# First loads of a fused attention and feed-forward kernel on one queue, with one warming matmul less

## The chip, the cores and the metric

One core of one Trainium2 chip. The metric is device time in microseconds (us) of one execution; the time given for a kernel is a median over runs. The profile is of one execution, and its span runs from the first to the last instruction.

Five engines run side by side, each with its own list of instructions, and meet by semaphores: TensorE (PE in the profile, PEld for its weight loads), VectorE (DVE), ScalarE (ACT), GpSimd (POOL) and SyncE (SP). SyncE and ScalarE also issue DMA transfers, each on a queue of its own (SPq and ACTq in the profile; q1 and q10 in its list of queues).

## The reference

The input x is 2048 rows by 512. A linear attention with 32 heads of width 16 and a feed-forward layer with 1376 hidden columns are both computed from it and mixed by a gate:

```
g = sigmoid((x * gate_w).sum(-1, keepdims=True))
q, k, v = heads(x @ wqkv)
phi(t) = concat(softmax(t @ w_phi), softmax(-(t @ w_phi)))     # per head, for q and k
kv, z = phi(k)^T v, phi(k) summed over rows
a = (phi(q) @ kv / (phi(q) @ z + 1e-6)) @ wo
b = relu(x @ w1) @ w2
out = g * a + (1 - g) * b
```

All inputs and the output are bf16.

## The kernel before, in words

Rows are worked on in tiles of 128 (16 of them) and in chunks of 512 (4 of them). The hidden layer h = relu(x @ w1) is made transposed, in 11 blocks of 128 hidden columns for each chunk. The products q and k use weights that are folded with w_phi first: `pe_fold` (L408) multiplies a transposed weight (WT, which the DMA transposes wkT and wqT fill) by a block-diagonal mask of w_phi (WBD, made on VectorE at L363 from the load wphi).

Each piece of work is a named task with an engine, the tasks that it depends on, and a closure that emits its instructions. The order on each engine is written out by hand in the table `ORDER` at the top: a list of task names for each engine. A task waits only for the semaphores of its dependencies; everything behind a waiting task on its engine waits with it. `emit` puts the waits and the instructions out in that order. The fields `dur` and `lat` belong to a planner that isn't run here, and do nothing.

The start of the program is what the change touches. The names:

- `warm0` (L292), on PE: six matmuls of 512 columns on a constant, into a PSUM bank that is overwritten later. They wait for nothing but the constant.
- `x00` to `x03` (issued at L306): the four 128-row tiles of x's first chunk, 128 KB each, into a piece of the tile FT (it is called XN in the code). `xt00`, `xt01` and so on (L384) transpose each tile on PE by the identity matrix, two 128-column blocks a task. `xe00`, `xe10`, `xe20`, `xe30` (L396, ScalarE) and `xe01` to `xe31` (L399, VectorE) evict those to XT.
- `w1a0` to `w1a3` (L306): the four 128-row blocks of w1, each cut to its first 512 columns, 128 KB each, into the tile W1 (the profile shortens names, so W1 and W2 both appear as W there). `w1b` is columns 512 to 1023 of all four row blocks, `w1c` the rest.
- `hh00`, `hh01` (row block 0, tile 0 and tile 1 of x), `hh1` (row block 1), `hh2` (row block 2), `hh3` and `hh4` (row block 3, two halves), all at L439: the first part of h on PE, for the first 256 rows of x. `hh00` and `hh01` have four matmuls of 128 columns each, `hh1` and `hh2` four of 256, `hh3` and `hh4` two of 256. `hr0`, `hr1` and `h0_0` to `h0_3` (L445) finish those four column blocks, `h0_4` and on (L425) do whole blocks; `h0_4` is the first to need `w1b`.
- `f1_0` to `f1_3` (L408): the folds for k, which need `wkT` and the masks. `h1_0` (L425) is the first matmul group that needs `x1`, the DMA transpose (L311) of x's second chunk, and `x1` is issued only when `w1c` has landed.

PE's order there is: warm0, xt00, xt01, xt10, xt11, hh00, hh01, hh1, hh2, xt20, xt21, hh3, xt30, xt31, hh4, hr0, hr1, h0_0 to h0_5, f1_0 to f1_3, h0_6. SyncE issues x00, w1a0, w1a2, x02, x03, w1b, wphi, wkT, w1c, wv, x1 and on; ScalarE begins with x01, w1a1, w1a3 and then the evictions. Before ScalarE's first activation there is a table load (ACT_TABLE_LOAD in the profile), which stands where that activation stands.

Of the kernel before, what the change touches and what calls it, by code (L numbers as in the profile page):

```python
# [5 lines left out]
ACT = mybir.ActivationFunctionType  # L6
# [9 lines left out]

ORDER = {
# [4 lines left out]
    ),  # L22
# [5 lines left out]
    ),  # L28
    "act": (
# [153 lines left out]
def bass_gated_mix__linear_kernel_hedgehog__dense_activation_relu__prompt_kernel(  # L183
# [11 lines left out]
    x2 = A_x.rearrange("b s d -> (b s) d")  # L195
# [4 lines left out]
    P = 128  # L200
# [14 lines left out]
    NPH, NOM, NOT, NOS = 7, 3, 4, 5  # L215
    NDB, AB = (6, 7), (3, 4, 5, 2)
    GATE_LIMIT = 40.0
    WARM = (6 * (512,),)
    RL = 400.0
    FE = "dve"  # L220

    with ExitStack() as es:
        E = es.enter_context

        def sb(name, shape, dt):
            return E(nc.sbuf_tensor(name, shape, dt))
# [6 lines left out]
        W1 = sb("W1", [P, ND, W1C], BF16)  # L233
# [30 lines left out]
        EP = sb("EP", [P, NT], FP32)  # L264
# [7 lines left out]
        def psap(off, dims):  # L272
# [3 lines left out]
        add = g.add  # L276
# [5 lines left out]
            boost=700.0)  # L282
# [4 lines left out]
        one = nc.const_aps.tensor(1.0, (P, 1), BF16).tensor  # L287
        ones_w, ones_m = (bass.AP(tensor=one, offset=0, ap=[[1, P], [0, n]]) for n in (P, 512))

        def pe_warm(q, cols):  # L290
            for n in cols:
                last = q.matmul(PS[:, 2, 0:n], ones_w, ones_m[:, 0:n], start=True, stop=True)  # L292
            return last

        for n, cols in enumerate(WARM):
            add(f"warm{n}", "pe", lambda q, c=cols: pe_warm(q, c), (), dur=sum(cols) / 1200.0, boost=3000.0)
# [3 lines left out]
        def after_last(name, eng):  # L300
            if eng in queue:
                g.follow(queue[eng], name)
            queue[eng] = name

        def load(name, eng, out_, in_, deps=(), dur=0.1, lat=6.0, **how):
            add(name, eng, lambda q: q.dma_start(out=out_, in_=in_, **how), deps, dur=dur, lat=lat, dma=True,  # L306
                boost=1e4)
            after_last(name, eng)
# [9 lines left out]
        w1r = B_w1.rearrange("(j p) n -> p j n", p=P)  # L318
        x0r = x2[chunk(0), :].rearrange("(m p) d -> p m d", p=P)
        wvr = A_wqkv[:, 2 * D:3 * D].rearrange("(j p) n -> p j n", p=P)  # L320
        def load_x(m, eng, lat):
            load(f"x0{m}", eng, XN[:, m, :], x0r[:, m, :], dur=0.45, lat=lat)

        def load_w(j, eng, lat):
            load(f"w1a{j}", eng, W1[:, j, 0:512], w1r[:, j, 0:512], dur=0.45, lat=lat)

        load_x(0, "sp", 2.95)
        load_x(1, "act", 3.1)
        load_w(0, "sp", 3.2)
        load_w(1, "act", 3.4)  # L330
        load_w(2, "sp", 3.8)
        load_w(3, "act", 3.95)
        load_x(2, "sp", 4.0)
        load_x(3, "sp", 3.9)
        load("w1b", "sp", W1[:, :, 512:1024], w1r[:, :, 512:1024], dur=0.5, lat=5.0)
# [52 lines left out]
        for m in range(4):  # L388
# [3 lines left out]
            for n, eng in enumerate(("act", "dve")):  # L392
                xo = XT[:, 2 * n:2 * n + 2, m * P:(m + 1) * P]
                xi = PS[:, XB[m][n], 0:2 * P].rearrange("p (j t) -> p j t", j=2)
                if eng == "act":
                    add(f"xe{m}{n}", eng, lambda q, o=xo, i=xi: q.activation(o, i, ACT.Copy), (f"xt{m}{n}",), dur=0.35,  # L396
                        boost=9000.0 - 10 * m)
                else:
                    add(f"xe{m}{n}", eng, lambda q, o=xo, i=xi: q.tensor_copy(o, i), (f"xt{m}{n}",), dur=0.37,  # L399
                        boost=9000.0 - 10 * m)  # L400
# [36 lines left out]
        def pe_h_first(q, j, c0, c1, ks=range(4)):  # L437
            for k in ks:
                last = q.matmul(PS[:, GB4[k], c0:c1], W1[:, j, k * P:(k + 1) * P], XT[:, j, c0:c1],  # L439
                                start=(j == 0 and c0 == 0), stop=(j == ND - 1), skip_group_check=True)  # L440
            return last
# [11 lines left out]
        prev = "hh01"  # L453
        for n, (j, ks) in enumerate(((1, range(4)), (2, range(4)), (3, (0, 1)), (3, (2, 3)))):
            add(f"hh{n + 1}", "pe", lambda q, j=j, ks=ks: pe_h_first(q, j, 0, 2 * P, ks),
                (f"xe0{j // 2}", f"xe1{j // 2}", f"w1a{j}", prev), dur=0.11 * len(ks), boost=8500.0)
            prev = f"hh{n + 1}"

        for k in range(2):
            add(f"hr{k}", "pe", lambda q, k=k: pe_h_rest(q, k, 2 * P, 3 * P, True), ("xe20", "xe21", prev), dur=0.22,  # L460
                boost=8200.0)
            prev = f"hr{k}"
# [13 lines left out]
        for n, (kind, a, k) in enumerate(units):  # L476
            b = GB4[n] if n < 4 else FB[2] if n == 4 else HB[(n - 4) % len(HB)]
            if kind == "h":
                halved = n < 4
                deps = [*xof[a], *w1of[k], prev, *freed[b]]  # L480
                if k == KT - 1:
                    deps.append("gw")
                    add(f"h{a}_{k}", "pe", lambda q, a=a, b=b: pe_h_tail(q, a, b), deps, dur=0.69)
                    prev = f"h{a}_{k}"
# [15 lines left out]
                    deps, dur=(0.22 if k < 2 else 0.44) if halved else 0.87,  # L500
                    boost=8000.0 if n < 3 else 0.0)
                prev = f"h{a}_{k}"
# [3 lines left out]
            else:  # L506
                deps = ["wqT", *wbd, prev, *freed[b]]
                add(f"f{a}_{k}", "pe", lambda q, a=a, k=k, b=b: pe_fold(q, a, k, b), deps, dur=0.24, boost=1000.0)
                prev = f"f{a}_{k}"
# [4 lines left out]
        for j in range(ND):  # L514
# [3 lines left out]
                boost=1800.0)  # L518
# [11 lines left out]
        for m in range(NT):  # L530
            def add(*a, boost=20.0 * (len(widths) * 2 - m // 2 - VLAG), **how):
                return g.add(*a, boost=boost, **how)
# [17 lines left out]
        for jn, (kind, tiles) in enumerate(jobs):  # L550
# [66 lines left out]
            else:  # L617
# [4 lines left out]
                    dur=0.11 + 0.207 * w)  # L622
# [24 lines left out]
                for m in tiles:  # L647
# [39 lines left out]
                    if m == NT - 1:  # L687
# [3 lines left out]
                        prev = None  # L691
                        for h2 in range(2):
# [12 lines left out]
                            prev = f"a{m}_{h2}"  # L705
# [12 lines left out]
                            else:  # L718
                                add(f"oe{m}_1", "dve", lambda q, m=m, b=b, cs=cs: q.tensor_scalar(  # L719
                                    OSB[:, m % NOS, cs], PS[:, b, 0:cs.stop - cs.start], OMG[:, m:m + 1], None, ALU.mult), need,  # L720
                                    dur=0.4)
                            add(f"st{m}_{h2}", ("act", "sp")[h2], lambda q, m=m, cs=cs: q.dma_start(
                                out=o2[m * P:(m + 1) * P, cs], in_=OSB[:, m % NOS, cs]), (f"oe{m}_{h2}",), dur=0.5,
                                lat=1.5, dma=True)
# [55 lines left out]
```

## Time and profile before

| | us |
|---|---|
| median of 3 runs | 150.16 (150.09 to 150.39) |
| the profiled execution | 149.87 |
| its span | 148.3 |
| TensorE busy | 145.5 |
| VectorE busy | 111.7 |
| GpSimd busy | 109.6 |
| ScalarE busy | 91.4 |

How to read it: the busy times are of single engines and overlap. "L292" is a line of the kernel. In a list in order of time, a row gives the start, the length of the stretch, the engine (with a q for its sequencer, which issues DMAs), the line, the operation, the tile written and the tiles read, the number of instructions merged into the row, and in brackets the idle time of the engine ahead of it with what ended it. The ends of matmuls are modelled and overlap the next start, so the starts are the safer numbers. For a DMA the duration on the issuing engine is the time to issue it; the time from there to its landing is listed in another view, the DMA view.

### The profile page before, as it was taken

What the parts mean: (1) busy time and instruction counts of PE and PEld (TensorE: products, weight loads), DVE (VectorE), ACT (ScalarE), POOL (GpSimd) and SP (SyncE); (2) the same over time, 40 slices, a digit from 0 to 9 for tenths busy, and PEclk for the clock granted to TensorE, in tenths of its full rate; (3) what the DMA queues carried; (4) which work ended last, traced back from release to release, by engine and by line L of the source; (5) the groups of instructions that cost most, each with busy time, mean ns of one, the idle gap of its engine ahead of it and who ended that gap; (6) DMA issues with size and microseconds to landing.
All of it is one profiled execution on the core that took longest, in us unless ns stands there. A gap on an engine that the chain in (4) does not pass through costs nothing.

```text
span 148.3 us, 2542 instructions
## 1 busy us (share of the span) xinstructions
PE 145.5 (98%) x1009; PEld 75.3 (51%) x1009; DVE 111.7 (75%) x169; ACT 91.4 (62%) x126; POOL 109.6 (74%) x72
## 2 busy tenths in 40 slices
PE   7999999999999999999999999999999999999994
PEld 2875444445654475445444545455444444445453
DVE  2433666998896948989999997999999988634502
ACT  3475769799969765898983937175583751310141
POOL 4000499999999999999999999999999793150000
PEclk9999999999999999999999999999999999999999
DMA  4998999910040001000000093646957785556752
GB/s 139 324 256 220 169 187 214 340 51 4 0 73 0 0 4 38 0 0 4 0 0 0 7 141 71 141 95 138 183 119 167 180 214 116 141 134 158 64 157 92
DMA packets 46363, 16.11 MB, mean 109 GB/s; under 512 B 39856, under 2 KB 46352, under 8 KB 46352
## 3 DMA queue, kind: packets, MB, share of 16 engines
q1 hardware_dynamic: 43760, 13.61, 42.6%
q10 hardware_dynamic: 2592, 2.34, 4.9%
q8 instruction: 8, 0.13, 0.4%
q14 instruction: 3, 0.02, 0.1%
HBM read 4.41 MB, written 2.10 MB: 44 GB/s over the span
## 4 chain that ended last, share of the span: by engine, by line
PE 98%; DVE 0%; issue 0%
PE PS L676 24%; PE PS L425 21%; PE PS L545 19%; PE PS L526 9%; PE PS L682 9%; PE PS L611 3%; PE PS L654 3%; PE PS L433 2%; PE PS L292 2%; PE PS L698 2%; PE PS L439 2%; PE PS L445 1%; PE PS L408 1%; PE PS L384 1%; PE PS L709 1%; DVE OSB L719 0%
## 5 line engine op out<-in xcount | busy, mean ns | idle before, releaser
L590 POOL TENSOR_TENSOR TS<-PB,MX 128x1024 bf16<-128x1024 bf16 (+1 forms) x18 | 30.9, 1723 | 14.5 <-DVE MX L581 14.5
L676 PE MATMUL PS<-W,HT 128*128 128x512 bf16 (+1 forms) x165 | 38.1, 379 | 0.0
L597 DVE TENSOR_REDUCE ZB<-FT 128x128 f32<-128x2048 bf16 (+1 forms) x18 | 36.6, 2031 | 1.8 <-ACT FT L595 1.8
L595 ACT ACTIVATE FT<-TS 128x2048 bf16<-128x2048 bf16 (+1 forms) x18 | 30.9, 1718 | 9.6 <-POOL TS L590 9.5
L425 PE MATMUL PS<-XT,W 128*128 128x512 bf16 x144 | 34.7, 379 | 0.0
L590 POOL TENSOR_TENSOR TS<-MN,PB 128x1024 bf16<-128x1024 bf16 (+1 forms) x18 | 30.9, 1726 | 0.8 <-DVE MN L583 0.8
L545 PE MATMUL PS<-WP,XT 128*128 128x512 bf16 x128 | 30.6, 379 | 0.0
L604 POOL TENSOR_TENSOR FT<-FT,SC 128x2048 bf16<-128x2048 bf16 (+1 forms) x9 | 29.6, 3293 | 0.0
L503 ACT ACTIVATE HT<-PS 128x512 bf16<-128x512 f32 x40 | 22.6, 597 | 5.4 <-PE PS L425 4.6
L581 DVE TENSOR_REDUCE MX<-PB 128x64 bf16<-128x1024 bf16 (+1 forms) x18 | 19.5, 1085 | 5.9 <-ACT PB L577 5.9
L676 PEld LDWEIGHTS PS<-W,HT 128*128 128x128 bf16 (+1 forms) x165 | 15.4, 98 | 16.9
L730 ACT ACTIVATE OSB<-PS,OMG 128x512 bf16<-128x512 f32 x14 | 9.6, 686 | 21.1 <-PE PS L682 20.5
L583 DVE TENSOR_REDUCE MN<-PB 128x64 bf16<-128x1024 bf16 (+1 forms) x18 | 19.3, 1084 | 3.2 <-ACT PB L577 3.2
L425 PEld LDWEIGHTS PS<-XT,W 128*128 128x128 bf16 x144 | 13.7, 98 | 15.4
L577 ACT ACTIVATE PB<-PS 128x1024 bf16<-128x1024 f32 (+1 forms) x18 | 16.7, 927 | 7.2 <-PE PS L545 4.0
L545 PEld LDWEIGHTS PS<-WP,XT 128*128 128x128 bf16 x128 | 12.1, 98 | 13.5
L526 PE MATMUL PS<-WV,XT 128*128 128x512 bf16 x64 | 16.4, 379 | 0.0
L627 POOL TENSOR_TENSOR FT<-FT,SR 128x1024 bf16<-128x1024 bf16 (+1 forms) x9 | 15.7, 1740 | 0.7
L682 PE MATMUL PS<-WO,OT 128*128 128x512 bf16 x60 | 14.9, 378 | 0.0
L663 DVE SCALAR_TENSOR_TENSOR OTM<-PS,EG,RD 128x256 bf16<-128x256 f32 x32 | 13.8, 463 | 0.2
L661 DVE RECIPROCAL RD<-PS 128x16 f32<-128x16 f32 x32 | 6.4, 232 | 9.0 <-PE PS L654 8.8
L535 ACT ACTIVATE VS<-PS 128x512 bf16<-128x512 f32 x16 | 9.6, 602 | 4.3 <-PE PS L526 4.3
(55 smaller groups left out, 106.6 us busy)
## 6 DMA issues: line engine op xcount, KB each, us to landing
out_dram<-OSB ACTq DMA_DIRECT2D x14, 128.0 KB, 2.2
W<-in_B_w_dram SPq DMA_DIRECT2D x1, 1280.0 KB, 7.5
W<-in_B_w_dram SPq DMA_DIRECT2D x1, 512.0 KB, 4.5
WV<-in_A_wqkv_dram SPq DMA_DIRECT2D x1, 512.0 KB, 4.9
WO<-in_A_wo_dram SPq DMA_DIRECT2D x1, 512.0 KB, 7.5
FT<-in_A_x_dram SPq DMA_DIRECT2D x3, 128.0 KB, 3.1
W<-in_B_w_dram SPq DMA_DIRECT2D x1, 352.0 KB, 4.1
W<-in_B_w_dram ACTq DMA_DIRECT2D x2, 128.0 KB, 3.3
```

The source lines that it names most:

```text
L425: last = q.matmul(PS[:, b, :], W1[:, j, k * P:(k + 1) * P], XT[:, j, chunk(c)], start=(j == 0), stop=(j == ND - 1))
L503: add(f"rl{a}_{k}", "act", lambda q, a=a, k=k, b=b: q.activation(HT[:, k, chunk(a)], PS[:, b, :], ACT.Relu), (prev,), dur=0.6, boost=RL)
L526: last = q.matmul(PS[:, 2, :], XT[:, j, m * P:(m + 1) * P], WV[:, j, :], start=(j == 0), stop=(j == ND - 1))
L545: last = q.matmul(PS[:, n, :], XT[:, j, m * P:(m + 1) * P], WP[:, s, j, :], start=(j == 0), stop=(j == ND - 1))
L581: add(f"mx_{J}", "dve", lambda q, sl=sl, w=w, i=pbg: q.tensor_reduce(MX[:, sl, 0:w * H], i, AX.X, ALU.max), (f"ev_{J}", old("t1")), dur=0. ...
L583: add(f"mn_{J}", "dve", lambda q, sl=sl, w=w, i=pbg: q.tensor_reduce(MN[:, sl, 0:w * H], i, AX.X, ALU.min), (f"ev_{J}", old("t2")), dur=0. ...
L590: add(f"{tn}_{J}", "pool", lambda q, o3=o3, a3=a3, b3=b3: q.tensor_tensor(o3, a3, b3, ALU.subtract), (f"{'mx' if sg == 0 else 'mn'}_{J}", ...
L595: add(f"ex_{J}", "act", lambda q, fs=fs, ts=ts, w=w: q.activation(FT[:, fs, 0:w * F], TS[:, ts, 0:w * F], ACT.Exp), (f"t1_{J}", f"t2_{J}", ...
L597: add(f"sm_{J}", "dve", lambda q, fs=fs, sl=sl, w=w: q.tensor_reduce(ZB[:, sl, 0:2 * w * H], FT[:, fs, 0:w * F].rearrange("p (g d) -> p g ...
L604: add(f"nm_{J}", "pool", lambda q, f3=f3, sl=sl, w=w: q.tensor_tensor(f3, f3, SC[:, sl, 0:2 * w * H].unsqueeze(2).to_broadcast([P, 2 * w * ...
L676: last = q.matmul(PS[:, ab, :], HT[0:r, k, m * P:(m + 1) * P], W2[0:r, k, :], start=(k == 0), stop=False)
L682: last = q.matmul(PS[:, ab, :], OT[:, m % NOT, t, :], WO[:, t, :], start=False, stop=(t == ND - 1))
```

## The change

SyncE issues all of the first loads, and ScalarE none. w1a2 and w1a3 become one load of 256 KB, which keeps the name w1a2; hh3 and hh4 wait for it as hh2 does. SyncE's order is then x00, x01, w1a0, w1a1, w1a2, x02, x03, w1b, and the rest as it was. ScalarE begins with a new task, `first`: an activation that copies one column of a constant into a column of EP, which is written again before it is read. It waits for nothing. warm0 has five matmuls instead of six.

```diff
     "sp": (
-        "x00 w1a0 w1a2 x02 x03 w1b wphi wkT w1c wv x1 x2 wqT x3 gw w2a w2b wo hx0 hx1 hx2 tq0 tq1 "
+        "x00 x01 w1a0 w1a1 w1a2 x02 x03 w1b wphi wkT w1c wv x1 x2 wqT x3 gw w2a w2b wo hx0 hx1 hx2 tq0 tq1 "
...
     "act": (
-        "x01 w1a1 w1a3 xe00 xe10 xe20 xe30 rl0_0 rl0_1 rl0_3 rl0_2 rl0_4 fe1_1 fe1_3 rl0_5 ev_k0 rl0_8 rl0_6 "
+        "first xe00 xe10 xe20 xe30 rl0_0 rl0_1 rl0_3 rl0_2 rl0_4 fe1_1 fe1_3 rl0_5 ev_k0 rl0_8 rl0_6 "
...
-    WARM = (6 * (512,),)
+    WARM = (5 * (512,),)
...
         load_x(0, "sp", 2.95)
-        load_x(1, "act", 3.1)
+        load_x(1, "sp", 3.1)
         load_w(0, "sp", 3.2)
-        load_w(1, "act", 3.4)
-        load_w(2, "sp", 3.8)
-        load_w(3, "act", 3.95)
+        load_w(1, "sp", 3.4)
+        load("w1a2", "sp", W1[:, 2:4, 0:512], w1r[:, 2:4, 0:512], dur=0.45, lat=3.8)
+        add("first", "act", lambda q: q.activation(EP[:, 0:1], bass.AP(tensor=one, offset=0, ap=[[1, P], [1, 1]]), ACT.Copy),
+            (), dur=1.5)
+        after_last("first", "act")
         load_x(2, "sp", 4.0)
         load_x(3, "sp", 3.9)
...
-                (f"xe0{j // 2}", f"xe1{j // 2}", f"w1a{j}", prev), dur=0.11 * len(ks), boost=8500.0)
+                (f"xe0{j // 2}", f"xe1{j // 2}", f"w1a{min(j, 2)}", prev), dur=0.11 * len(ks), boost=8500.0)
```

## The prediction

> **What bounds the kernel now.** I read first the page's busy shares and slices, then the chain of waits, then TensorE's row and the two DMA-issuing engines in order of time over the first 13 us, then the DMA view by stage and by single issue.
>
> ```profile
> PE 145.5 (98%) x1009; PEld 75.3 (51%) x1009; DVE 111.7 (75%) x169; ACT 91.4 (62%) x126; POOL 109.6 (74%) x72
> ...
> PE 98%; DVE 0%; issue 0%
> ```
>
> TensorE (PE) is busy from 0.77 us to the end, and the chain that ended last is PE alone. So the end moves only by what moves PE's row. The change touches its first microseconds:
>
> ```profile
> 0.77 2.72 PE L292 MATMUL PS<-const-bfloat16-1.0 128*128 128x512 bf16 x6 [0.77 <-PEq L765]
> 3.58 1.01 PE L384 MATMUL PS<-IDN,FT 128*128 128x128 bf16 x8
> 4.43 1.98 PE L439 MATMUL PS<-XT,W 128*128 128x128 bf16 x16
> 6.24 0.39 PE L384 MATMUL PS<-IDN,FT 128*128 128x128 bf16 x4
> ...
> 10.73 0.44 PE L408 MATMUL PS<-WBD,WT 128*128 128x128 bf16 x5
> ```
>
> Six warming matmuls (L292), the transposes of x00 and x01 (L384), hh00 to hh2 (L439), x02's transposes (6.24), and wkT's folds (10.73). The columns are start, duration and what ran. In the chain the first eight transposes take 1.01 us, 0.126 each, the next four 0.22, 0.055 each: PE starts at half rate. The granted-clock column reads 1.00 throughout and doesn't show this; the pace does. The switch lies inside hh1, whose four 256-column matmuls take 0.55 us (5.26, worked out below, to 5.81, which is 6.24 less hh2's 4 x 0.109): at half rate they would take 0.85, at full rate 0.44, so the first 0.23 us is slow and full rate begins at **5.49**. Idle time before that costs half; after it, all.
>
> ```profile
> 0.74 0.40 SPq L306 DMA_DIRECT2D FT<-in_A_x_dram  x1
> 1.20 0.89 SPq L306 DMA_DIRECT2D W<-in_B_w_dram  x2
> 2.13 0.91 SPq L306 DMA_DIRECT2D FT<-in_A_x_dram  x2
> 3.08 0.43 SPq L306 DMA_DIRECT2D W<-in_B_w_dram  x1
> 3.55 0.51 SPq L306 DMA_DIRECT2D WPS<-in_A_w_phi_dram  x1
> 4.11 3.27 SPq L311 DMA_TRANSPOSE WT<-in_A_wqkv_dram  x1
> ```
>
> SyncE issues x00, w1a0, w1a2, x02, x03, w1b, wphi, wkT: five loads from 0.74 to 3.08, **0.47 us each**. ScalarE issues x01, w1a1, w1a3 beside them:
>
> ```profile
> 0.74 0.41 ACTq L306 DMA_DIRECT2D FT<-in_A_x_dram  x1
> 1.18 0.94 ACTq L306 DMA_DIRECT2D W<-in_B_w_dram  x2
> 2.15 1.28 ACT L396 ACT_TABLE_LOAD   x1 [2.15 <-issue]
> 3.99 0.81 ACT L396 ACTIVATE XT<-PS 128x256 bf16<-128x256 f32 x2 [0.56 <-PE PS L384]
> ```
>
> From issue to landing the DMA view gives x00 2.7, x01 2.9, w1a0 2.9, w1a1 3.2, w1a2 3.2, w1a3 3.4, x02 3.2, x03 3.1, w1b 4.5, wkT 5.4 us. So x00 lands at 3.44, x01 3.64, w1a3 5.07, wkT 9.5. The first transpose starts at 3.58, 0.14 after x00; that 0.14 is my step from a landing to PE. By stage, in columns window, PE busy, clock, DMA share, GB/s:
>
> ```profile
> 1.70:2.30 0.60, 0.60 (x3) 1.00 0.41 41
> 2.30:2.80 0.50, 0.50 (x2) 1.00 0.83 291
> 2.80:3.30 0.50, 0.50 (x2) 1.00 1.09 377
> 3.30:5.10 1.80, 1.71 (x16) 1.00 1.09 378
> ```
>
> From 2.8 on the engines are full: 128 KB costs 0.35 us while two queues feed them. One queue supplies 128 KB per 0.47 us, which is less.
>
> **The change part by part.**
>
> *One warming matmul less.* The sixth starts at 2.86 and takes 0.43 (the spacing of the warming starts). It goes, but PE then waits for x00. The idle stretch before the first transpose, 0.25 us now, becomes longer; the matmul itself did no work. Nothing is gained unless x00 lands before 3.29 - 0.14 = 3.15.
>
> *x01 goes to the second place on SP.* x00 no longer shares the engines with x01. By 2.3 us 25 KB had moved (0.6 x 41), by 2.8 another 145 KB; x00's remaining 106 KB at 377 GB/s end about 2.6 instead of about 2.9. So x00 lands at 3.44 (no gain) to 3.1; I take 3.2, since the 377 row is its nearest. PE's first transpose: 3.34, 0.24 early. x01 is issued at 1.20 and lands 0.47 behind x00, 3.67 (by its bare lag of 2.7, 3.9). Its transposes start at 3.81 instead of 3.96: PE idles 0.09 there.
>
> *w1a0 and w1a1 slip by one and two places* (issues 1.67, 2.14): landings 4.14 and 4.60. hh00 needs xe00, done by then, and w1a0: 4.14 + 0.14 = 4.28, against 4.43. hh01 needs xe10, which ended at 4.80, 0.84 behind x01's first transpose; now 4.65, so hh01 starts at 4.71, against 4.86, and hh1 at 5.13, against 5.26 (0.40 behind hh01). Gain at hh1 0.13 us, at half rate: **0.07 us** of work.
>
> *w1a2 and w1a3 as one load* saves one issue on a queue. Issue 2.61, landing 4.60 + 0.47 + 0.35 for the second block = 5.42. hh2's place is 5.74; the load has to land by 5.60. By the lag of 3.2 plus 0.35 it lands at 6.16, and hh2 waits 0.56, which costs 0.49 against now. I take 5.42, nearest to x03's landing 0.31 behind x02 on a queue that had the engines alone; both ends stay for the range. x02 (3.08) then lands at 5.8, x03 at 6.1; their places on PE are 6.17 and 6.62: no wait.
>
> *Everything behind on SP* issues two places, 0.94 us, later: w1b at 4.02, lands by 8.5, needed by the matmul group at 9.00; wphi by 8.8, its four masks on VectorE end about 9.8; wkT issued at 5.05, lands by 10.45, needed at 10.66: 10.59 with the step, **0.07 us to spare**. x1 (issued at 11.56 behind w1c, lag 5.7) by 18.2, needed at 18.46: 0.12 to spare. Its successors are used many microseconds after. If these transfers slip by 0.3 more, PE waits some 0.2 us at full rate.
>
> *ScalarE's table load* moves from 2.15 to about 0.75 behind a one-column activation. Neither is on the path: it ends at 3.43 now, and the first eviction waits for PE until 3.99. Cost and gain nothing; the cover is 0.56 us.
>
> *Sum:* 149.87 - 0.07 = 149.80 in terms of the profiled execution (span 148.3 and 1.57 around it). The median shown is 0.29 above that execution, so the forecast is 150.16 - 0.07 = 150.09, say **150.1 us**. Its own range is 149.9 to 150.3.
>
> The Trainium skill ("DMA: Bandwidth & Descriptors", Issuing engines are not separate DMA queues) says that issuing from several engines saves only the sequencer's issue time, usually small beside the transfer. Here the issue, 0.47 us, is longer than a load's share of the engines, 0.35, so the trace doesn't bear out the word small. By that rule x01 and w1a0 would follow x00 every 0.35 us, hh1 would be some 0.25 early, and the sum would be 150.0.
>
> **The rivals.**
>
> *A: the loads in line come too late (slower).* A single queue at 0.47 us per load leaves w1a2's 256 KB too late for hh2. It decides from a landing at 5.60. For it: w1a1 to x03 all took 3.1 to 3.4; w1b, also many rows per partition, took 4.5. Against it: those lags were measured with both queues filling the engines. Price 0.2 to 0.5 us: **150.3 to 150.7**, about 150.55. A late wkT (from 10.52) or x1 costs 0.2 of the same kind, and is partly the same wait.
>
> *B: the full rate comes later (slower).* PE's row before 5.49 has idle time of 0.25 us before x00 and little else; with five warming matmuls it is 0.48 (2.86 + 0.43 = 3.29 becomes 2.86, start at 3.34) plus 0.09 and 0.04. If full rate needs an unbroken stretch, 4.72 us from 0.77 to 5.49, and the longer pause starts it anew at 3.34, it comes at 8.06: 2.57 us more at half rate, 1.3 us: **151.4**. It decides from a pause longer than 0.25 us. For it: the pause doubles. Against it: 0.25 us was tolerated, and 0.48 is still short beside 4.7.
>
> The Trainium skill ("TensorE: Matmul & The Clock Gate", Part 1: The HAM clock gate) describes a free-running window of 3.4 us that has to be busy; missing it would move the switch to 8.9 and, as an estimate, cost 1.7 us, 151.9. The trace shows that the switch came 4.7 us after the first matmul, which fits such a window and doesn't give its threshold.
>
> *C: x00 comes much earlier (faster by over 0.2%).* If the slow stretch of 41 GB/s is the two queues starting against each other, x00 may land at 2.7 and PE start 0.7 early at half rate: 0.35 us, **149.8**. Against it: the loads behind are spaced by the issue, so that PE would wait for them again.
>
> **How the numbers follow.** A measurement of this kernel can tell about 0.2%, 0.3 us, from no change. Forecast, with the back-to-back variant and a load that is only slightly late: 0.54. A beyond 0.3 us: 0.20. B: 0.13. C: 0.13. So faster 0.13, same 0.54, slower 0.33. The range 149.7 to 150.8 holds the forecast, nearly all of A and most of C (0.04 of it lies lower); B is left out, some 0.19 in all.
>
> **What would show it.** PE's first transpose at 3.3 to 3.4 and x01's near 3.8; hh00 near 4.3; no idle time before 5.74 at hh2; L384's next four at about 6.17 and the folds (L408) at about 10.66. A wait of PE for L306's W at hh2 says A; warm-pace matmuls only after 5.5 says B. I am wrong if any landing comes over 0.2 us from mine with PE waiting for it, or if the rate changes at another time.

## The result, and the profile after

The change makes the kernel slower: 151.33 us against 150.37 us (medians of 8 runs each), a ratio of 1.0072 with a 95% interval of 1.0044 to 1.0100. The forecast was 150.1 us with a range of 149.7 to 150.8, so the time lies above the range, and the likeliest case, no difference, is not what happened.

The profiled execution took 151.95 us, its span is 150.4. It is one of the slower of its kernel's runs (150.87 to 152.13), the one shown of before, with 149.87, one of the faster (149.84 to 150.74). The two profiles lie 2.1 us apart, the medians 1.0. So the profile after shows where time went; how much is read from the runs. Ratios of this document leave out executions far above their kernel's fastest: two of before_four_small (395 and 871 us) and two of x23_scalar (153.1 and 154.1 us).

The chain that ended last no longer consists of PE alone (the changed kernel's page, shares of the span by engine):

```profile
PE 85%; DMA 7%; SPq 6%; issue 0%; DVE 0%
```

Of what PE waited for, longest first (name, total, times, longest, in us), the changed kernel shows four waits for transfers. The kernel before has only the first of these rows, the start of the program:

```profile
PE PS L292 <- PEq L767: 0.8, 1, 0.8
PE PS L427 <- DMA XT<-in_A_x_dram: 0.7, 1, 0.7
PE PS L386 <- DMA FT<-in_A_x_dram: 0.5, 1, 0.5
PE PS L441 <- DMA W<-in_B_w_dram: 0.4, 1, 0.4
PE PS L410 <- DMA WT<-in_A_wqkv_dram: 0.3, 1, 0.3
```

PE's row in order of time, from the first to the last of these waits. Lines below the change are two higher than before: L384 is now L386, L439 is L441, L425 is L427, L408 is L410.

```profile
0.77 2.29 PE L292 MATMUL PS<-const-bfloat16-1.0 128*128 128x512 bf16 x5 [0.77 <-PEq L767]
2.97 1.02 PE L386 MATMUL PS<-IDN,FT 128*128 128x128 bf16 x8
4.02 1.57 PE L441 MATMUL PS<-XT,W 128*128 128x128 bf16 x12
5.95 0.60 PE L441 MATMUL PS<-XT,W 128*128 128x256 bf16 x4 [0.36 <-DMA W<-in_B_w_dram]
...
7.53 0.40 PE L386 MATMUL PS<-IDN,FT 128*128 128x128 bf16 x4 [0.55 <-DMA FT<-in_A_x_dram]
...
12.00 1.05 PE L410 MATMUL PS<-WBD,WT 128*128 128x128 bf16 x16 [0.26 <-DMA WT<-in_A_wqkv_dram]
...
20.64 1.02 PE L427 MATMUL PS<-XT,W 128*128 128x512 bf16 x4 [0.68 <-DMA XT<-in_A_x_dram]
```

Set against the starts of before and those forecast, in us (h1_0's start before is the row at 17.66 plus four matmuls of 0.216):

| work on PE | before | forecast | after | late against before |
|---|---|---|---|---|
| first transpose (x00) | 3.58 | 3.34 | 2.97 | -0.61 |
| hh00 (w1a0) | 4.43 | 4.28 | 4.02 | -0.41 |
| hh2 (w1a2) | 5.81 | 5.74 | 5.95 | +0.14 |
| x03's transposes | 6.68 | 6.62 | 7.53 | +0.85 |
| folds (wkT) | 10.73 | 10.66 | 12.00 | +1.27 |
| h1_0 (x1) | 18.53 | 18.46 | 20.64 | +2.11 |

The lead of 0.6 us at the start was real, larger than forecast, and was gone at hh2. From there PE is later after each wait. But the waits don't add up. Each ends when its load has landed, whatever PE did before. The chain that ended last shows it for x1 (start, length, what; its pieces from the issue of wkT to PE):

```profile
5.10 4.73 SPq L311
9.88 4.84 DMA W<-in_B_w_dram
14.73 5.78 DMA XT<-in_A_x_dram
20.64 1.02 PE PS L427 x4
```

The issue of wkT holds up the issue of w1c, w1c's landing starts x1, and x1's landing starts h1_0; PE has no part in this chain before 20.64. So in this execution h1_0 would have begun at 20.64 without the three waits ahead of it, too: the last wait sets the 2.11 us, and that is the 2.1 us by which the spans differ.

SyncE's queue shows what came late:

```profile
4.06 0.44 SPq L306 DMA_DIRECT2D W<-in_B_w_dram  x1
...
5.10 4.73 SPq L311 DMA_TRANSPOSE WT<-in_A_wqkv_dram  x1
...
14.73 5.39 SPq L311 DMA_TRANSPOSE XT<-in_A_x_dram  x2
```

The issues of w1b and wkT are 1.0 us late, as forecast (0.94). But the issue of wkT takes 4.73 us instead of 3.27. The DMA view (size, then time from issue to landing) says the same of the loads: x00 and x01 land after 2.1 us (at 2.8 and 3.3), but x03 and w1b take longer than before:

```profile
FT<-in_A_x_dram SPq DMA_DIRECT2D x1, 128.0 KB, 3.9
W<-in_B_w_dram SPq DMA_DIRECT2D x1, 512.0 KB, 5.6
WT<-in_A_wqkv_dram SPq DMA_TRANSPOSE x1, 6.8
```

These are x03 (3.1 before), w1b (4.5) and wkT (5.4). So wkT lands at 11.9 instead of 9.5: 1.0 us from the later issue, 1.4 us from the longer way. By stage (window, PE busy, clock, DMA share, GB/s), the changed kernel and then the kernel before:

```profile
1.70:2.30 0.60, 0.60 (x3) 1.00 0.76 189
2.30:5.10 2.80, 2.77 (x20) 1.00 0.86 245
5.10:7.00 1.90, 1.52 (x14) 1.00 0.81 219
```

```profile
2.30:5.10 2.80, 2.71 (x18) 1.00 1.04 363
5.10:7.00 1.90, 1.90 (x23) 1.00 1.08 305
```

The changed kernel moves more until 2.3 us (189 GB/s against 41, the row shown with the prediction). From then to 5.1 us its engines move a third less, and they are not full after it, though w1b's 512 KB had been issued at 4.06.

### The profile page after: what moved, and what is told of

It reads as the page before. It is cut to its first block, busy times and chain, and to the rows that moved or that the text cites. A ratio compares the mean times of both kernels' runs of the same rounds, so it can differ in the third digit from the quotient of the medians.

```text
span 150.4 us, 2540 instructions
## 1 busy us (share of the span) xinstructions
PE 145.8 (97%) x1008; PEld 75.0 (50%) x1008; DVE 111.7 (74%) x169; ACT 91.5 (61%) x127; POOL 109.7 (73%) x72
## 4 chain that ended last, share of the span: by engine, by line
PE 85%; DMA 7%; SPq 6%; issue 0%; DVE 0%
PE PS L678 24%; PE PS L427 17%; PE PS L547 16%; PE PS L528 9%; PE PS L684 9%; DMA XT<-in_A_x_dram 4%; DMA W<-in_B_w_dram 3%; SPq L311 3%; PE PS L613 3%; PE PS L656 3%; SPq L306 3%; PE PS L435 2%; PE PS L700 2%; PE PS L410 1%; PE PS L711 1%
## 5 line engine op out<-in xcount | busy, mean ns | idle before, releaser
L427 PE MATMUL PS<-XT,W 128*128 128x512 bf16 x144 | 34.8, 379 | 0.7 <-DMA XT<-in_A_x_dram 0.7
L427 PEld LDWEIGHTS PS<-XT,W 128*128 128x128 bf16 x144 | 13.7, 98 | 16.3 <-ACT PB L579 1.1
L547 PEld LDWEIGHTS PS<-WP,XT 128*128 128x128 bf16 x128 | 12.1, 98 | 13.5
```

Of the source, the lines that this page charges most:

```text
L427: last = q.matmul(PS[:, b, :], W1[:, j, k * P:(k + 1) * P], XT[:, j, chunk(c)], start=(j == 0), stop=(j == ND - 1))
L547: last = q.matmul(PS[:, n, :], XT[:, j, m * P:(m + 1) * P], WP[:, s, j, :], start=(j == 0), stop=(j == ND - 1))
```

## The experiments

Theory after the result: the move of the loads to one queue is the whole cause; it makes what stands behind them on SyncE late, x03, w1b, wkT and x1, and PE waits. Rivals: the warming matmul or ScalarE's early activation has part in it; the later issue alone explains it; the 256 KB load explains it; the landings vary from one execution to the next and the kernel before merely has the spare time. Ratios are to the kernel before on the same chip, with the 95% interval.

**loads_alone.** The changed kernel with six warming matmuls and without `first`.

```diff
-        "first xe00 xe10
+        "xe00 xe10
-    WARM = (5 * (512,),)
+    WARM = (6 * (512,),)
```

> The changed kernel with six warming matmuls again and without the early activation on ScalarE: the move of the loads alone. Theory (the line of loads on one queue is the whole cause): as the changed kernel, 0.7 to 1.3 us above the kernel before, PE waiting for w1a2, x03, wkT and x1. Rival (the warming matmul or the table load carry part of it): under 0.5 us above it.

151.33 us, ratio 1.0090 (1.0061 to 1.0119). wkT lands 7.0 us after its issue at 5.09, at 12.1, and PE starts the folds at 12.21, 1.5 us later than before; the span, 149.8, is 1.5 us longer too.

```profile
12.21 1.05 PE L407 MATMUL PS<-WBD,WT 128*128 128x128 bf16 x16 [0.32 <-DMA WT<-in_A_wqkv_dram]
```

The loads are the whole cause; fewer warming matmuls and the early activation save nothing of it. As x1 landed in time here, its wait is not a necessary part.

**before_two_small and before_four_small.** The kernel before with two or four loads of 2 KB into an unused tile, which only push SyncE's later issues back by 0.95 or 1.9 us.

```diff
-        "x00 w1a0 w1a2 x02 x03 w1b
+        "x00 w1a0 w1a2 x02 x03 d0 d1 w1b
+        SPARE = sb("SPARE", [P, 2, 8], BF16)
+        for n in range(2):
+            load(f"d{n}", "sp", SPARE[:, n, :], x2[n * P:(n + 1) * P, 0:8], dur=0.45, lat=2.0)
```

> The kernel before, both queues as they were, with two extra loads of 2 KB each into an unused tile on SyncE's queue just ahead of w1b: SyncE's later issues slip by two places, and hardly a byte is added. Theory (the slip of wkT and x1 on SyncE costs the time): 0.5 to 1.2 us above the kernel before, with PE waiting for wkT or x1 and for nothing earlier. Rival (one queue alone feeds the engines worse, and the slip is covered by 0.07 to 0.12 us of spare time and more): within 0.2 us of it.

> The kernel before with four extra loads of 2 KB instead of two on SyncE ahead of w1b: a slip of four places, 1.9 us. Theory (spare time of the loads behind, then one for one): wkT lands near 11.4 to 11.6 and f1 waits; 1.0 to 1.5 us above the kernel before, where two small loads gave 0.5. Rival (the slip matters little beside the one queue): 0.4 to 0.7 us.

Two: 150.55 us, 1.0028 (1.0005 to 1.0052). Four: 150.51 us, 1.0031 (1.0012 to 1.0049). The folds' wait is there in both, and w1b takes 4.5 and 4.2 us, no more than in the kernel before. With two:

```profile
5.06 3.55 SPq L311 DMA_TRANSPOSE WT<-in_A_wqkv_dram  x1
```

```profile
10.74 1.05 PE L411 MATMUL PS<-WBD,WT 128*128 128x128 bf16 x16 [0.18 <-DMA WT<-in_A_wqkv_dram]
```

With four, wkT is issued at 6.00 and the wait is 0.26, at 11.32. The profile with two is of its fastest execution (149.83 us), so its wait of 0.18 us does not account for the 0.3%. So a slip of two places costs 0.3%, under half of what the change costs with the same slip (by the medians; the intervals just overlap), and it doesn't grow one for one: with four places wkT's issue takes 3.15 us. My expectation for four (1.0 to 1.5 us) was wrong, and with it the idea that the slip of the issues is the whole cause.

**x1_no_wait.** The changed kernel with x1 not behind w1c.

```diff
-        load_t("x1", XT[:, :, chunk(1)], x2[chunk(1), :], ("w1c",), 2.6, 2.3)
+        load_t("x1", XT[:, :, chunk(1)], x2[chunk(1), :], (), 2.6, 2.3)
```

> The changed kernel with x1 issued without waiting for w1c to land. Theory (x1's lateness is the last of the waits and the others are folded into it): x1 is issued some 3 us earlier, the wait for it goes and 0.5 to 0.8 us of the loss with it, the waits for w1a2, x03 and wkT stay. Rival (x1 lands no earlier, since its transfer shares the engines with w1c and wv): as the changed kernel.

151.13 us, 1.0074 (1.0044 to 1.0104): the loss stays. In its profile the wait for x1 is gone; x03, w1a2 and wkT are still waited for:

```profile
PE PS L386 <- DMA FT<-in_A_x_dram: 0.8, 1, 0.8
...
PE PS L441 <- DMA W<-in_B_w_dram: 0.5, 1, 0.5
PE PS L410 <- DMA WT<-in_A_wqkv_dram: 0.3, 1, 0.3
```

wkT lands at 12.1 and the folds start at 12.19, as in loads_alone. The wait for x1 in the profile after belongs to that execution.

**x23_scalar.** The changed kernel with x02 and x03 on ScalarE's queue.

```diff
-x00 x01 w1a0 w1a1 w1a2 x02 x03 w1b
+x00 x01 w1a0 w1a1 w1a2 w1b
-        "first xe00
+        "first x02 x03 xe00
```

> The changed kernel with x02 and x03 issued by ScalarE behind its early activation, so that w1b, wkT and x1 have their former places on SyncE. Theory (the slip): the waits for wkT and x1 go, and the time comes to within 0.3 us of the kernel before, or below it by up to 0.3 us, since x00 lands early. Rival (the first loads on one queue are the harm): still 0.5 us or more above it, with the wait for w1a2.

152.28 us, 1.0120 (1.0064 to 1.0176), the slowest by its median. I had meant x02 and x03 to be issued after the activation, at about 2.2 us. ScalarE's row shows otherwise:

```profile
0.74 1.28 ACT L332 ACT_TABLE_LOAD   x1 [0.74 <-PEq L767]
0.81 0.87 ACTq L306 DMA_DIRECT2D FT<-in_A_x_dram  x2
2.04 0.20 ACT L332 ACTIVATE EP<-const-bfloat16-1.0 128x1 f32<-128x1 bf16 x1
```

They are issued at 0.81 and 1.22, and moved ahead of x01, w1a0 and w1a2, which PE needs first; hh2 starts at 7.15. PE also keeps half rate until about 8.7 us: hh2's four matmuls take 0.81 us, in the changed kernel 0.43. So this run tried another order of the loads, and says nothing on the slip.

**before_merged and line_unmerged.** The 256 KB load alone, in the kernel before; and the changed kernel without it.

```diff
-        load_w(2, "sp", 3.8)
-        load_w(3, "act", 3.95)
+        load("w1a2", "sp", W1[:, 2:4, 0:512], w1r[:, 2:4, 0:512], dur=0.45, lat=3.8)
```

```diff
-        load("w1a2", "sp", W1[:, 2:4, 0:512], w1r[:, 2:4, 0:512], dur=0.45, lat=3.8)
+        load_w(2, "sp", 3.8)
+        load_w(3, "sp", 3.95)
```

> The kernel before with only w1a2 and w1a3 merged into one load of 256 KB in w1a2's place on SyncE; ScalarE issues x01 and w1a1. No issue on SyncE slips. Theory M (the 256 KB load): w1b lands 5.6 us after its issue, near 8.7, and the time rises by 0.3 to 1.0 us. Theory L (one queue): w1b lands near 7.6 and the time is within 0.3 us of the kernel before.

> The changed kernel with w1a2 and w1a3 as two loads again, both on SyncE: eight loads in line ahead of w1b, so that w1b is issued 0.47 us later than in the changed kernel, near 4.53. In the changed kernel w1b landed 5.6 us after its issue, in the kernel before and in the one with two small loads 4.5 us. Theory M (the 256 KB load is what makes the loads behind it late): w1b lands 4.5 us after its issue, near 9.0, SyncE's issue of wkT ends there, wkT lands near 11.1, and the time is 0.3 to 0.7 us above the kernel before. Theory L (loads from one queue alone are what makes them late): w1b takes 5.6 us again, lands near 10.2, and the time is 1.2 to 1.8 us above it.

before_merged: 150.27 us, 1.0010 (0.9993 to 1.0027), w1b after 4.3 us. line_unmerged: 151.44 us, 1.0088 (1.0056 to 1.0119), w1b after 5.2 us, wkT at 11.8. The merged load is harmless, and leaving it out of the line doesn't help.

**before_two_warm.** The kernel before with two warming matmuls, which opens a long pause ahead of x00.

```diff
-    WARM = (6 * (512,),)
+    WARM = (2 * (512,),)
```

> The kernel before with two warming matmuls instead of six: PE pauses for some 2 us ahead of x00 instead of 0.25. Theory (PE goes to full rate after a window of some 3.4 us without a long pause, as the runs so far show it between 4.6 and 8.8 us): the full rate comes 2 to 3 us later, 1.0 to 1.7 us slower. Rival (the warming matmuls do nothing for the rate): within 0.3 us.

151.49 us, 1.0095 (1.0072 to 1.0118). The row of PE's transposes and hh groups keeps half rate until nearly 9 us:

```profile
3.44 1.01 PE L384 MATMUL PS<-IDN,FT 128*128 128x128 bf16 x8 [1.66 <-DMA FT<-in_A_x_dram]
...
8.13 0.63 PE L384 MATMUL PS<-IDN,FT 128*128 128x128 bf16 x4
8.56 0.61 PE L439 MATMUL PS<-XT,W 128*128 128x256 bf16 x2
8.99 1.95 PE L445 MATMUL PS<-XT,W 128*128 128x128 bf16 x24
```

Four transposes take 0.63 us there, 0.39 at full rate. So warming does bring the full rate forward, here by some 3 us and 1.4 us of time. In the changed kernel the pause was only 0.11 us (2.86 to 2.97, since x00 came at 2.8), and rival B of the prediction had no occasion.

**before_again1, before_again2.** The kernel before, profiled twice more.

> The kernel before, unchanged, profiled again, to see how its loads spread from one execution to the next. In the six profiles with all first loads on SyncE or ScalarE's share cut to late loads, w1b landed 5.2 to 6.2 us after its issue, in the profiles of the kernel before, with the merged load and with two small loads 4.3 to 4.5, in the one with two warming matmuls 5.5. Theory (the queue alone decides): 4.3 to 4.6 us, wkT lands near 9.5. Rival (it varies with the execution, and spare time hides it in the kernel before): 5 us or more, wkT lands by 10.7, and PE waits at most 0.2 us for it.

> The kernel before once more, for the same question: by the theory w1b lands 4.3 to 4.6 us after its issue, by the rival 5 us or more in at least one of the two.

149.82 and 149.56 us, one run each. The first of them has w1b after 5.3 us and wkT after 6.5, at 10.6:

```profile
4.09 4.31 SPq L311 DMA_TRANSPOSE WT<-in_A_wqkv_dram  x1
```

```profile
10.68 1.05 PE L408 MATMUL PS<-WBD,WT 128*128 128x128 bf16 x16
```

The second has 4.8 and 5.8 (9.9). So in three executions wkT landed at 9.5, 9.9 and 10.6, and PE waited for it in none. The rival is right in this much: the landings vary by a microsecond, and the kernel before has just the room for it.

**w1b_scalar.** The changed kernel with w1b on ScalarE's queue, behind its second eviction.

```diff
-x02 x03 w1b wphi
+x02 x03 wphi
-        "first xe00 xe10 xe20
+        "first xe00 xe10 w1b xe20
```

> The changed kernel with w1b issued by ScalarE behind its second eviction, near 4.2 us, so that SyncE's issue of wkT doesn't stand behind w1b in the queue. Theory (wkT's issue is held until w1b is through, 9.83 against a landing of w1b at 9.70): the issue of wkT ends by 8.3, PE's wait for wkT goes, and the time is 0.3 to 1.0 us below the changed kernel; the waits for w1a2 and x03 stay. Rival (the engines are the limit, whichever queue w1b is on): wkT lands near 11.9 as in the changed kernel and the time stays.

151.52 us, 1.0102 (1.0073 to 1.0130). wkT's landing and the time are as the rival had them: wkT is issued at 4.54 and its issue lasts 5.41 us, until 9.95, while w1b lands at 10.1, now on the other queue. So it isn't w1b's place ahead of wkT in SyncE's queue that holds wkT up. PE does not wait for wkT in this profile, though: x02 took 4.4 us instead of 3.1, and the wait for it, 0.89 us at 7.51, is PE's last; the folds start at 12.28, after wkT's landing at 12.1.

**line_x23_merged, line_five, x01_scalar.** All loads in line but fewer of them: x02 and x03 as one load of 256 KB (a slip of one place); in addition w1a0 and w1a1 as one (no slip). And the changed kernel with x01 back on ScalarE (a slip of one place).

```diff
-x00 x01 w1a0 w1a1 w1a2 x02 x03 w1b
+x00 x01 w1a0 w1a1 w1a2 x02 w1b
+        load("x02", "sp", XN[:, 2:4, :], x0r[:, 2:4, :], dur=0.45, lat=4.0)
```

```diff
-x00 x01 w1a0 w1a1 w1a2 x02 w1b
+x00 x01 w1a0 w1a2 x02 w1b
+        load("w1a0", "sp", W1[:, 0:2, 0:512], w1r[:, 0:2, 0:512], dur=0.45, lat=3.3)
```

```diff
-x00 x01 w1a0 w1a1 w1a2 x02 x03 w1b
+x00 w1a0 w1a1 w1a2 x02 x03 w1b
-        "first xe00
+        "x01 first xe00
```

> The changed kernel with x02 and x03 as one load of 256 KB as well: six loads in line, w1b issued near 3.55, a slip of one place. Theory (the engines run out of work between the issues): the rate from 5.1 to 7.0 us rises above 220 GB/s, wkT lands by 11.2, and the time is 0.3 to 0.7 us above the kernel before. Rival (one queue alone is slow): wkT near 11.8, 0.9 to 1.4 us above it.

> The changed kernel with w1a0 and w1a1 as one load too: x00, x01, and three loads of 256 KB, five issues ahead of w1b, as many as SyncE has in the kernel before, so that w1b is issued near 3.1 and nothing slips, all on one queue. hh00 waits for 256 KB, near 4.9, mostly at half rate. Theory (issues too slow to keep the engines full): from 2.3 to 5.1 us the rate is over 290 GB/s, wkT lands by 10.7, the time is within 0.5 us of the kernel before. Rival (one queue alone is slow): under 270 GB/s, wkT after 11.2, 0.7 us or more above it.

> The changed kernel with x01 issued by ScalarE ahead of its early activation; SyncE has six loads in line ahead of w1b, a slip of one place. Theory (issue pace): x00 lands near 3.3 again, the loads behind stay in a line of 0.47 us each, wkT lands near 11.0 to 11.5, 0.3 to 0.9 us above the kernel before. Rival (a second queue at the start is what matters): wkT by 10.6 and within 0.3 us.

line_x23_merged: 150.59 us, 1.0032 (1.0013 to 1.0051). x01_scalar: 150.68 us, 1.0039 (1.0021 to 1.0057). line_five: 151.68 us, 1.0092 (1.0056 to 1.0127). By the medians a slip of one place instead of two halves the loss, in either way (the intervals touch that of the changed kernel). In the profiles of the two wkT still lands at 11.9 and 11.7; but both are of executions at the slow end of their runs (151.15 and 151.02 us), and theory and rival aren't told apart by them.

line_five has w1b issued at 3.15 and wkT at 10.6, at the upper end of what the kernel before shows. So without a slip one queue gives wkT in time, and its stage from 5.1 on is full:

```profile
2.30:5.10 2.80, 1.91 (x13) 1.00 0.90 262
5.10:7.00 1.90, 1.90 (x14) 1.00 1.01 332
```

But the first stage stays poor, 262 GB/s, against the theory's 290, and the time is lost elsewhere:

```profile
4.93 2.72 PE L439 MATMUL PS<-XT,W 128*128 128x128 bf16 x16 [0.89 <-DMA W<-in_B_w_dram]
7.45 0.63 PE L384 MATMUL PS<-IDN,FT 128*128 128x128 bf16 x4
```

hh00 waits 0.89 us for the 256 KB, and after this pause PE is still at half rate at 8.3 us, as rival B described.

**merged_x02_scalar.** An attempt at a better kernel: two queues, the merged load, x02 on ScalarE, so that SyncE has one load fewer.

```diff
-        "x00 w1a0 w1a2 x02 x03 w1b
+        "x00 w1a0 w1a2 x03 w1b
-        "x01 w1a1 w1a3 xe00
+        "x01 w1a1 x02 xe00
```

> The kernel before with w1a2 and w1a3 merged on SyncE and x02 moved to ScalarE, behind w1a1: SyncE has one load fewer ahead of w1b, so that wkT is issued 0.47 us earlier than before; ScalarE has three loads as before. Theory (the spare time of wkT and x1 decides, and PE is busy without a break once it is enough): 0 to 0.4 us below the kernel before. Rival (the merged load delays hh2, or x02 comes late on ScalarE): 0.1 to 0.4 us above it.

150.56 us, 1.0020 (1.0004 to 1.0037): not better. wkT is issued 0.44 us earlier than before, but takes 7.0 us and lands at 10.7, and hh2 waits 1.27 us for w1a2 in the profile. None of these kernels beats the one before.

The landings of w1b and wkT side by side, one profile each:

| kernel | queues | slip, places | w1b, us from issue | wkT lands | ratio |
|---|---|---|---|---|---|
| before, three profiles | two | 0 | 4.5, 5.3, 4.8 | 9.5, 10.6, 9.9 | 1 |
| before_two_warm | two | 0 | 5.5 | 10.7 | 1.0095 |
| before_merged | two | 0 | 4.3 | 9.4 | 1.0010 |
| before_two_small | two | 2 | 4.5 | 10.6 | 1.0028 |
| before_four_small | two | 4 | 4.2 | 11.2 | 1.0031 |
| line_five | one | 0 | 5.3 | 10.6 | 1.0092 |
| line_x23_merged | one | 1 | 6.1 | 11.9 | 1.0032 |
| changed | one | 2 | 5.6 | 11.9 | 1.0072 |
| loads_alone | one | 2 | 5.8 | 12.1 | 1.0090 |
| x1_no_wait | one | 2 | 5.8 | 12.1 | 1.0074 |
| line_unmerged | one | 3 | 5.2 | 11.8 | 1.0088 |
| w1b_scalar | one load (w1b) on the second | 1 | 6.2 | 12.1 | 1.0102 |
| x01_scalar | one load on the second | 1 | 5.9 | 11.7 | 1.0039 |
| x23_scalar | two loads on the second | 0 | 5.9 | 11.1 | 1.0120 |
| merged_x02_scalar | two | -1 | 5.8 | 10.7 | 1.0020 |

Some of these ratios have another cause beside: the half rate of PE (before_two_warm, line_five, x23_scalar) and earlier waits (hh00 in line_five, hh2 in x23_scalar and merged_x02_scalar, x02 in w1b_scalar). wkT lands by 11.2 wherever at least two loads are on ScalarE's queue, whatever the slip, and after 11.6 in every kernel with at most one load there and a slip. In all 17 profiles it lands 1.9 to 2.3 us after w1b. In the five kernels with the line of loads where PE's last wait is for wkT (loads_alone, x1_no_wait, line_unmerged, line_x23_merged, x01_scalar) the folds start 1.1 to 1.5 us later than in the profile before, and each span is longer by the same, to 0.1 us. So it is with two and four small loads (0.0 and 0.6 us).

The rate from 2.3 to 5.1 us parts the kernels more clearly than w1b's way does: 238 to 267 GB/s in the seven profiles with all loads ahead of w1b in line, 293 to 363 in the eight with two queues (241 and 244 in x01_scalar and x23_scalar).

## Why the prediction was wrong

*What bounds the kernel:* right. PE was the chain, and each wait on PE after full rate counted in full.

*One warming matmul less, and the table load:* right in size, nothing. loads_alone puts both back and is no faster.

*x01 on SP's second place, w1a0 and w1a1 behind:* right in direction, too small. x00 came at 2.8 instead of 3.2, and hh00 was 0.41 us early instead of 0.15. The loads followed each other by 0.5 to 0.6 us.

*Rival C* was half right: x00 landed at 2.8, 0.1 after its 2.7, PE started 0.61 early, and the slow stretch of 41 GB/s became 189. What stood against it was right too: PE waited for the loads behind, and the lead was gone at hh2. That two queues starting together make the stretch slow is not shown: x23_scalar issues from both, from 0.74 and 0.81 on, and its x00 lands after 2.1 us as well.

The Trainium skill ("DMA: Bandwidth & Descriptors", Issuing engines are not separate DMA queues) had said that a second issuing engine saves only issue time; its variant of the sum was 150.0. The changed kernel's loads did not follow at the engines' pace of 0.35 us, and the rate from 2.3 to 5.1 us was 245 GB/s against 363, so the trace disagrees with taking that saving for small here.

*w1a2 as one load:* I took a landing of 5.42 and needed 5.60; it came at 5.8 (issued at 2.60, 3.2 later), so hh2 waited. This is rival A's place, at less than its price: hh2 started 0.21 us after the forecast's 5.74.

*Everything behind on SP:* **this is the step that failed.** I counted the slip of the issues, 0.94 us, and let the landings follow one for one: "wkT issued at 5.05, lands by 10.45, needed at 10.66", 0.07 us to spare with the step. The issue was right (5.10), the landing was 11.9. The term that I had at 0.94 us measured 2.4 us between the two profiles: 1.0 of slip and 1.4 of a longer way, 6.8 us from issue to landing instead of 5.4. Most of the longer way is w1b's: it took 5.6 us instead of the 4.5 that I kept, and wkT landed 2.2 us after it (1.9 before). x1 had the same 0.94 us in the sum and was issued 3.2 us later (14.73 against 11.56), behind wkT's issue and a w1c that took 4.8 us instead of 4.1. Against the slowest of the three profiles of before, with 6.5, the longer way is 0.3, and the whole term 1.3. Two mistakes are in it. I took one profile's lags for constants, though they vary by 1.1 us in the same kernel. And I held the later loads to the lags of two queues, though I had just worked out that one queue supplies less.

*Rival A* was the right mechanism, at the wrong price. I priced it at hh2, with 0.2 to 0.5 us, and gave a late wkT or x1 0.2 us, "partly the same wait". That they are partly the same wait was right: the later wait takes up the earlier ones. But the later one was the dear one, 1.3 us at the folds and 2.1 at h1_0 in the profile after, 1.5 at the folds in loads_alone. Its chance, 0.20, was too small as the spare time of 0.07 and 0.12 us was written down beside a lag known to a tenth at best.

*Rival B* did not occur in the changed kernel, which has full rate from about 5.1 us. (The pause of before, 0.25 us in the text, is 0.29 by its own working, 3.29 to 3.58.) In before_two_warm, line_five and x23_scalar full rate came only between 8.6 and 9.0 us. But a pause does not decide alone: in line_unmerged PE was idle for 0.40 us ahead of hh00, at 4.43, and hh00 to hh2 took 1.60 us, against 1.98 before and 2.72 in line_five. The Trainium skill ("TensorE: Matmul & The Clock Gate", Part 1: The HAM clock gate) gives a free-running window of 3.4 us that must be busy. With two warming matmuls full rate came near 8.9 us, about 5.5 after the pause ended at 3.44, which lies between the 3.4 and 6.8 us that such a window would give, as an estimate.

What is shown: the loads alone cost the time (loads_alone); neither the merged load (before_merged) nor x1's wait (x1_no_wait) is needed for it; the slip alone costs 0.3% (two and four small loads), the line with the same slip 0.7 to 0.9%. In the profiles the last wait sets how late PE is. What stays open is why less is moved from one queue. Loads of 256 KB, which should have kept the engines supplied, gave 262 GB/s in line_five, where loads_alone has 267 without them. And w1b took as long on ScalarE's queue (6.2 us), and 5.8 us in merged_x02_scalar, which uses two queues.

## What to carry to other kernels

A load moved onto another queue delays all that is queued behind it; where a consumer there has less spare time than the landings vary between executions, count on the wait. Waits for loads that do not depend on the waiting engine don't add up: price the one that lands latest against its need, also when it stands far down the queue. An earlier start is worth nothing when the third or fourth load behind it comes later than before. Profile the kernel before two or three times when the sum hangs on a tenth of a microsecond.

## What the hardware did that I had not expected

- ScalarE issues a DMA ahead of an activation that stands before it in its program: at 0.81 us, with the table load running from 0.74 to 2.02 and the activation at 2.04 (x23_scalar). In w1b_scalar w1b was issued at 3.87, while the first of the two evictions ahead of it, from 3.44 on, had barely ended.
- The issue of the DMA transpose wkT ends within 0.2 us of w1b's landing in every profile, whichever queue w1b is on: it ended at 7.4, 8.4, 7.8 in the three profiles of before, and w1b landed at 7.6, 8.4, 7.9; 9.8 and 9.7 in the changed kernel, 9.95 and 10.1 in w1b_scalar. The load wphi, issued between them on SyncE, lands at about that time too (9.95 in the changed kernel, 10.4 in w1b_scalar), so what the issue waits for is not shown.
- The full rate of PE begins at different times in the same program: by the pace of the matmuls near 5.5, 5.2 and 4.2 us in the three profiles of before. In other kernels it came near 3.6 (merged_x02_scalar, where the first eight transposes took 0.64 us) and after 8.3 us (line_five).
